# Agent attention and two expert layers: a first block of 384 tokens, another order of the first loads, and a written order from the sums to the first folded slices

## The chip, the cores and the metric

The kernel runs on one core of a Trainium2 chip. The metric is the device time of one execution in microseconds (us), the median of several runs.

## The reference, cut to what matters

```python
def attention(q, k, v, agents):                  # 12480 tokens, width 128, 49 agents, float32
    a2k = softmax(agents @ k.T / sqrt(128))      # 49 x 12480
    agent_v = a2k @ v                            # 49 x 128
    q2a = softmax(q @ agents.T / sqrt(128))      # 12480 x 49
    return q2a @ agent_v                         # 12480 x 128

x = attention(q, k, v, agents)
h = x @ w_in1                                    # 128 -> 2048
x = where(h > 0, h, exp(min(h, 0)) - 1) @ w_out1 # 2048 -> 128
h = x @ w_in2
out = (max(h, 0) + alpha * min(h, 0)) @ w_out2
```

## The kernel before, in words

The tokens are cut into 25 blocks (`BLOCKS`, L23: ten of 480, fifteen of 512). Before any block can start, the kernel must have the 49 rows of agent values. The **prologue** (L438) makes them. It reads k in ten pieces (`PIECES`, L24), computes scores per piece (S, `scores`, L471), the maximum over the first five pieces and over the last five (D and X), subtracts it and takes exp (E, `weigh`, L506), and sums the values (A, `values`, L514, the matmuls of L521). In parallel it brings in the four expert matrices in 16 slices of 512 KB (w0 to w15) and **decodes** each (`decode`, L327): the words of a slice become a high and a low float32r part by about five operations on DVE (L344 to L353), some on ACT (L340, L363, L406) and some on POOL (L373 to L409). Slices 0 to 3 are the first matrix, 4 to 7 the second; then the third and fourth matrix alternate.

After the sums A9 the two halves are put together and divided (`cs`, `avs`, `rs`, L545 to L562), turned (L564) and copied to `avn` and `avq` (L568 to L571). Then the agent values are **folded** into the first expert matrix: four slices j, each with matmuls (L578, L583), two copies by ACT to `hi` (L584, L585) and two operations on DVE (L586, L590). The result `s1`, `s1q` is the stationary side of the first layer, so that the attention's second half and the first layer are one matmul per tile of 128 hidden columns.

For each block, the **query steps** (`Q_STEPS`, L270, 17 steps) make the softmax over the agents; the last, `q_place` (L261), copies parts of it across partitions by five DMAs, on the ACT queue for block 0 and on the SP queue for all others. Then **slots** follow (`slot`, L703). One call handles two units `u` (a unit is two of a block's 16 hidden tiles, 8 units per block): the first layer `g1` (L609, L612), its activation (L619, L620, L627, L629, L636, L638), the second layer `g2` into the bank `y`, and ten units later (`L2`) the third and fourth layer, `g3` and `g4`, the latter into the bank `o`. All large products are split into three float32r matmuls (`mm3`, L431).

What sets the order: SP's queue runs in the order in which the program emits (`PINNED`). `pump` (L288) issues the loads in the order of `LOADS` (L35); it stops at the first item whose ring has no free buffer. The rings are 9 tiles for k and v and `RAW` = 6 buffers for w; a w buffer comes free with the fifth DVE operation of its decode, a k tile with its scores, a v tile with its sums. `ORDER` (L39) writes out the prologue's steps; T2 advances the decodes by two pieces (`micro`, L415), Q2 makes two query steps of block 0. For the other engines a planner, with its own model of times, orders instructions by priority, which follows the program's order but for `high_priority`: 20 for S, D, X, E and A, and `URGENT` = 400 for all from `cs` to the fourth folded slice. From slot 12 on (`AUTO`) every engine runs in program order. In the slots each of four `ask` calls (L714) advances the decodes by `MICRO` = 2 pieces. From the fold on a decode takes its PSUM scratch by `spare` (L410) from the one bank `o`, which `g4` of block 0 needs too.

Of the kernel before, what the change touches and what calls it, by code (L numbers as in the profile page):

```python
# [8 lines left out]
F32 = mybir.dt.float32  # L9
# [13 lines left out]
BLOCKS = [480] * 10 + [512] * 15  # L23
# [10 lines left out]
RAW = 6  # L34
# [4 lines left out]
    k0 q0 w0 k1 k2 w1 k3 k4 w2 k5 k6 w3 k7 k8 w4 k9 v0 w5 v1 v2 w6 v3 v4 w7 v5 v6 w8 v7 v8 w9 v9 a0 q1  # L39
# [3 lines left out]
    S0 T2 S1 Q2 T2 S2 Q2 S3 T2 Q2 S4 D0 Q2 T2 S5 X0 E0 Q2 S6 T2 E1 Q2 S7 E2 T2 S8 Q2 E3 T2 Q2 S9 D1 E4 A0 X1 A1 T2  # L43
    E5 A2 E6 T2 A3 E7 A4 E8 T2 A5 E9 T2 A6 T2 A7 T2 A8 T2 A9 Q1 T2
# [3 lines left out]
URGENT = 400  # L48
# [8 lines left out]
def agent_attention_moe_kernel(  # L57
# [378 lines left out]
    w1 = {}  # L436

    def prologue():  # L438
# [6 lines left out]
        nc.vector.tensor_scalar(out=low, in0=low, scalar1=-1.0, scalar2=None, op0=ALU.mult)  # L445
        stages = [f for k in sorted(Q_STEPS) for f in Q_STEPS[k]]
        with tc.tile_pool(name="att", bufs=1) as att:
            att2 = att
            with tc.tile_pool(name="kv", bufs=KV) as kv:
                rings["kv"] = kv  # L450
                across = bank("o", 1)
                S = att.tile([P, 10, 10, A], F32, name="S")
                pm = att.tile([P, 2, A], F32, name="pm")
                top = att.tile([P, 10, A], F32, name="top")
                mc = att.tile([A, 2], F32, name="mc")
                mb = att.tile([A, P], F32, name="mb")
                mx = {}
                for j in range(4):
                    w1[j] = att.tile([P, 4, P], F32, name=f"w1_{j}")
                pump()  # L460

                for t in range(2):
                    nc.scalar.copy(out=agd[:, t, :], in_=agp[:, :A])
                nc.scalar.copy(out=ag1[:, 0, :], in_=agp)
                nc.vector.tensor_tensor(out=ag1[:, 1, :], in0=agp, in1=ag1[:, 0, :].bitcast(F32), op=ALU.subtract)
                nc.scalar.copy(out=ag2[:, 0, :], in_=agp)
                nc.vector.memset(ag2[:, 1, :].bitcast(F32), 0.0)
                ag = agd.rearrange("p t a -> p (t a)")
                av = {}

                def scores(i):  # L471
                    _, nch, m = PIECES[i]
                    sp = hpair()
                    s4 = sp[:m, :, :10 * A].rearrange("p b (c a) -> p b c a", a=2 * A)[:, :, :, :A]
                    for c in range(nch):
                        o = sp[:m, c // 5, 2 * A * (c % 5):2 * A * (c % 5) + 2 * A]
                        nc.tensor.matmul(o, kt[i][:, c * m:(c + 1) * m], ag, start=True, stop=True)  # L477
                    del kt[i]
                    free["kv"] += 1
                    pump()  # L480
                    parts = [(slice(0, 10), s4)]
                    if nch < 10:
                        parts = [(slice(0, 5), s4[:, :1]), (slice(5, nch), s4[:, 1:, :nch - 5])]
                    for cs, part in parts:
                        def shaped(x):
                            return x[:m, cs, :].rearrange("p (b c) a -> p b c a", b=part.shape[1])
                        nc.scalar.copy(out=shaped(S[:, i]), in_=part)
                        if i % 5:
                            last = S[:, i - 1] if i % 5 == 1 else top
                            nc.vector.tensor_tensor(out=shaped(top), in0=part, in1=shaped(last), op=ALU.max)  # L490
                    if i % 5 == 4:
                        nc.vector.tensor_reduce(
                            out=pm[:, i // 5, :], in_=top.rearrange("p c a -> p a c"), axis=AX.X, op=ALU.max
                        )

                def max_down(h):
                    tp = across[:A, P * (2 + h):P * (3 + h)]
                    nc.tensor.transpose(tp, pm[:, h, :], ident)
                    nc.vector.tensor_reduce(out=mc[:, h:h + 1], in_=tp, axis=AX.X, op=ALU.max)
                    nc.vector.tensor_copy(out=mb, in_=mc[:, h:h + 1].to_broadcast([A, P]))  # L500

                def max_across(h):
                    mx[h] = across[:, P * h:P * h + A]
                    nc.tensor.matmul(mx[h], mb, ident[:A, :A], start=True, stop=True)

                def weigh(i):  # L506
                    _, nch, m = PIECES[i]
                    nc.vector.tensor_tensor(
                        out=S[:m, i, :nch, :], in0=S[:m, i, :nch, :],
                        in1=mx[i // 5][:m, :].unsqueeze(1).to_broadcast([m, nch, A]), op=ALU.subtract,  # L510
                    )
                    nc.scalar.activation(out=S[:m, i, :nch, :], in_=S[:m, i, :nch, :], func=AF.Exp, scale=SCALE)

                def values(i):  # L514
                    _, nch, m = PIECES[i]
                    h, first, last = i // 5, i % 5 == 0, i % 5 == 4
                    if i == 0:
                        y = bank("y", 1)
                        av.update({n: y[:, 256 * n:256 * n + P + 1] for n in range(2)})
                    for c in range(nch):  # L520
                        nc.tensor.matmul(  # L521
                            av[h][:A, 0:P + 1], S[:m, i, c, :], vt[i][:m, c, :],
                            start=(first and c == 0), stop=(last and c == nch - 1),
                        )
                    del vt[i]
                    free["kv"] += 1
                    pump()

                def query(n):
                    for _ in range(n):  # L530
                        stages.pop(0)(0)

                does = {"S": scores, "D": max_down, "X": max_across, "E": weigh, "A": values, "Q": query, "T": micro}
                for x in ORDER.split():
                    if x[0] in "SDXEA":
                        with tc.high_priority(offset=PRIORITY):
                            does[x[0]](int(x[1:]))
                    else:
                        does[x[0]](int(x[1:]))
                assert not stages and all(i in done for i in range(4)), (stages, done, started)  # L540

                urgent = tc.high_priority(offset=URGENT)
                urgent.__enter__()

                cs = att.tile([A, 4], F32, name="cs")  # L545
                nc.vector.tensor_tensor(out=cs[:, 2:3], in0=mc[:, 0:1], in1=mc[:, 1:2], op=ALU.max)
                nc.vector.tensor_scalar(out=cs[:, 0:2], in0=mc, scalar1=cs[:, 2:3], scalar2=None, op0=ALU.subtract)
                nc.scalar.activation(out=cs[:, 0:2], in_=cs[:, 0:2], func=AF.Exp, scale=SCALE)
                avs = att.tile([A, 2, P + 1], F32, name="avs")
                nc.vector.tensor_scalar(  # L550
                    out=avs[:, 0, :], in0=av[0][:A, 0:P + 1], scalar1=cs[:, 0:1], scalar2=None, op0=ALU.mult
                )
                nc.vector.scalar_tensor_tensor(
                    out=avs[:, 1, :], in0=av[1][:A, 0:P + 1], scalar=cs[:, 1:2], in1=avs[:, 0, :],
                    op0=ALU.mult, op1=ALU.add,
                )
                rs = att.tile([A, 1], F32, name="rs")
                nc.vector.tensor_scalar(out=rs, in0=avs[:, 1, P:P + 1], scalar1=1e-9, scalar2=None, op0=ALU.add)
                nc.vector.reciprocal(out=rs, in_=rs)
                nc.vector.tensor_scalar(  # L560
# [13 lines left out]
            for j in range(4):  # L574
# [7 lines left out]
                for g in range(4):  # L582
                    nc.tensor.matmul(hq[32 * g:32 * g + 32, :], avq[:, g, :], w1[j][:, g, :], start=True, stop=True)  # L583
# [201 lines left out]
```

## Time and profile before

| | us |
|---|---|
| median of 3 runs | 1138.63 (1138.54 to 1139.36) |
| the profiled execution, whole time | 1139.54 |
| its span, first to last instruction | 1137.6 |
| PE busy in the span | 1087.1 (96%) |
| DVE busy | 863.8 (76%) |
| ACT busy | 804.1 (71%) |
| POOL busy | 612.3 (54%) |

PE is TensorE, DVE VectorE, ACT ScalarE, POOL GpSimd, SP SyncE; an engine's name with a q is its queue issuing DMAs. A busy time is a share of the whole span, so it hides that the first 160 us look quite unlike the rest. The matmuls' ends are modelled, so a busy PE is not always one at its peak.

### The profile page before, as it was taken

The numbers are of one execution on the slowest core, as the hardware profiler recorded it, in microseconds if no ns is written. First come the engines' busy times: TensorE is split into PE (matmuls) and PEld (weight loads), VectorE is DVE, ScalarE is ACT, GpSimd is POOL, SyncE is SP. The second block draws the span as 40 slices with busy tenths as digits, with TensorE's granted clock in tenths as the row PEclk, the third lists the DMA queues.
The fourth block names the chain that finished last, engine by engine and source line by source line (L and its number), as shares of the span: only waits on it lengthen the run. The fifth ranks groups of instructions, "written<-read, shape, count | busy, mean of one in ns | idle before, by whom it ended". The sixth has DMA issues, their size and how long they took to land.

```text
span 1137.6 us, 13427 instructions
## 1 busy us (share of the span) xinstructions
PE 1087.1 (96%) x5012; PEld 854.6 (75%) x5012; DVE 863.8 (76%) x995; ACT 804.1 (71%) x921; POOL 612.3 (54%) x340
## 2 busy tenths in 40 slices
PE   7677769999999999999999999999999999999998
PEld 7664558888888888877777777777777777777776
DVE  5679947878787878788787887878878778778653
ACT  3347637777877777777777777777777777877753
POOL 2326635655565556565555655665556555565440
PEclk9879679999999999999999999999999999999999
DMA  9940000000000000000000000000000000000000
GB/s 352 295 136 1 18 0 27 18 27 9 19 26 19 18 19 28 18 19 19 28 10 19 28 10 28 19 19 19 19 27 12 19 29 10 19 19 17 12 1 18
DMA packets 28978, 41.33 MB, mean 36 GB/s; under 512 B 3329, under 2 KB 19669, under 8 KB 28915
## 3 DMA queue, kind: packets, MB, share of 16 engines
q1 hardware_dynamic: 28719, 40.24, 11.5%
q8 instruction: 39, 0.64, 0.2%
q10 hardware_dynamic: 196, 0.25, 0.1%
q14 instruction: 24, 0.20, 0.1%
HBM read 27.60 MB, written 6.39 MB: 30 GB/s over the span
## 4 chain that ended last, share of the span: by engine, by line
PE 91%; DVE 4%; DMA 2%; ACT 2%; POOL 1%; issue 1%; SPq 0%; DVEq 0%; ACTq 0%; POOLq 0%
PE o L432 10%; PE o L434 9%; PE o L433 9%; PE h L433 8%; PE h L434 8%; PE h L432 8%; PE y L433 8%; PE y L432 8%; PE y L434 8%; PE h L609 8%; PE h L612 4%; PE y L521 2%; PE h L477 1%; DMA vt<-in_vm_dram 1%; DMA kt<-in_kT_dram 1%
## 5 line engine op out<-in xcount | busy, mean ns | idle before, releaser
L638 POOL TENSOR_TENSOR gl<-g,gh 128x1024 fp32r<-128x1024 f32 (+1 forms) x200 | 468.0, 2345 | 279.1 <-DVE gh L629 176.4
L669 DVE SCALAR_TENSOR_TENSOR xl<-h,xh 128x1024 fp32r<-128x1024 f32 (+1 forms) x200 | 239.6, 1198 | 144.8 <-ACT xh L668 143.4
L668 ACT ACTIVATE xh<-h 128x1024 fp32r<-128x1024 f32 (+1 forms) x200 | 201.2, 1006 | 193.1 <-PE h L434 192.6
L627 DVE SCALAR_TENSOR_TENSOR g<-e,h 128x1024 f32<-128x1024 f32 (+1 forms) x200 | 236.4, 1182 | 75.6 <-ACT e L620 54.9
L619 ACT ACTIVATE e<-h 128x1024 f32<-128x1024 f32 (+1 forms) x200 | 199.4, 997 | 36.5 <-PE h L612 33.3
L620 ACT ACTIVATE e<-e 128x1024 f32<-128x1024 f32 (+1 forms) x200 | 207.7, 1039 | 6.2
L432 PE MATMUL o<-xh,wo2h 128*128 128x512 f32 (+1 forms) x400 | 166.0, 415 | 0.4 <-DVE lin L394 0.4
L433 PE MATMUL y<-gl,wo1h 128*128 128x512 f32 (+1 forms) x400 | 157.5, 394 | 4.0 <-POOL gl L638 4.0
L432 PE MATMUL h<-yh,wi2h 128*128 128x512 f32 (+1 forms) x400 | 156.0, 390 | 2.7 <-ACT yh L656 2.7
L432 PE MATMUL y<-gh,wo1h 128*128 128x512 f32 (+1 forms) x400 | 157.4, 394 | 0.0
L433 PE MATMUL o<-xl,wo2h 128*128 128x512 f32 (+1 forms) x400 | 156.3, 391 | 0.7 <-DVE xl L669 0.7
L434 PE MATMUL y<-gh,wo1l 128*128 128x512 f32 (+1 forms) x400 | 156.8, 392 | 0.0
L434 PE MATMUL o<-xh,wo2l 128*128 128x512 f32 (+1 forms) x400 | 156.7, 392 | 0.0
L433 PE MATMUL h<-yl,wi2h 128*128 128x512 f32 (+1 forms) x400 | 156.3, 391 | 0.0
L434 PE MATMUL h<-yh,wi2l 128*128 128x512 f32 (+1 forms) x400 | 155.8, 389 | 0.0
L629 DVE SCALAR_TENSOR_TENSOR gh<-e,h 128x1024 fp32r<-128x1024 f32 (+1 forms) x100 | 118.8, 1188 | 0.0
L609 PE MATMUL h<-pst,s 128*128 128x512 f32 (+1 forms) x400 | 110.7, 396 | 5.6 <-DVE g L627 2.3
L636 ACT CAST gh<-g 128x1024 fp32r<-128x1024 f32 (+1 forms) x100 | 102.0, 1020 | 5.5 <-DVE g L627 5.5
L432 PEld LDWEIGHTS o<-xh,wo2h 128*128 128x128 f32 x400 | 75.7, 189 | 35.0 <-ACT xh L668 16.9
L609 PEld LDWEIGHTS h<-pst,s 128*128 128x128 f32 x400 | 75.2, 190 | 23.9 <-issue 2.6
L433 PEld LDWEIGHTS y<-gl,wo1h 128*128 128x128 f32 x400 | 76.1, 190 | 21.8 <-POOL gl L638 5.6
L432 PEld LDWEIGHTS h<-yh,wi2h 128*128 128x128 f32 x400 | 75.2, 188 | 18.9 <-ACT yh L656 2.9
(144 smaller groups left out, 1315.0 us busy)
## 6 DMA issues: line engine op xcount, KB each, us to landing
vt<-in_vm_dram SPq DMA_DIRECT2D x9, 640.0 KB
kt<-in_kT_dram SPq DMA_DIRECT2D x8, 640.0 KB
wi<-in_w_in_dram SPq DMA_DIRECT2D x8, 512.0 KB
wo<-in_w_out_dram SPq DMA_DIRECT2D x8, 512.0 KB
q<-in_qT_dram SPq DMA_DIRECT2D x15, 256.0 KB
psq<-pst SPq DMA_DIRECT2D x60, 64.0 KB
out_dram<-o SPq DMA_DIRECT2D x15, 256.0 KB
q<-in_qT_dram SPq DMA_DIRECT2D x10, 240.0 KB
```

What stands on the lines that cost most here:

```text
L432: nc.tensor.matmul(out, w_hi, x_hi, start=start, stop=False)
L433: nc.tensor.matmul(out, w_hi, x_lo, start=False, stop=False)
L434: nc.tensor.matmul(out, w_lo, x_hi, start=False, stop=stop)
L609: nc.tensor.matmul(h_t[u + v][:, c, :], s1[:, i + 2 * v + c, :], pst[b][:, :n], start=True, stop=False)
L619: nc.scalar.activation(out=e, in_=h_t[u], func=AF.Relu, scale=-1.0)
L620: nc.scalar.activation(out=e, in_=e, func=AF.Exp, scale=-1.0)
L627: nc.vector.scalar_tensor_tensor(out=g, in0=e, scalar=-1.0, in1=h, op0=ALU.add, op1=ALU.max)
L629: nc.vector.scalar_tensor_tensor(out=gh, in0=e, scalar=-1.0, in1=h, op0=ALU.add, op1=ALU.max)
L636: nc.scalar.copy(out=gh, in_=g)
L638: nc.gpsimd.tensor_tensor(out=gl, in0=g, in1=gh.bitcast(F32), op=ALU.subtract)
L668: nc.scalar.activation(out=xh, in_=h, func=AF.Relu)
L669: nc.vector.scalar_tensor_tensor(out=xl, in0=h, scalar=0.0, in1=xh.bitcast(F32), op0=ALU.max, op1=ALU.subtract)
```

## The change

The first block has 384 tokens, followed by six of 480 and eighteen of 512: 25 blocks as before. `LOADS` asks for w0 ahead of k0, and for w1 to w5 earlier among the k; `RAW` falls to 4. `ORDER` begins with one T2 and has one less at the end, and the last query step of block 0 (Q1) moves from the end to behind E6. `q_place` issues on SP for block 0 too. The tiles `w1`, `avn` and `avq` move to the permanent pool, `avq` keeps one copy instead of four, `hi` has one buffer, the output tile `o` one instead of two. What followed the sums becomes `normalize` and `fold(j)`; `normalize`, `fold(0)` and `fold(1)` stand in a region in which every engine keeps program order, without `URGENT`; `fold(2)` and `fold(3)` come behind slot 0, and slot 0 advances no decode. The bodies of the prologue's steps only lose indentation.

```diff
-BLOCKS = [480] * 10 + [512] * 15
+BLOCKS = [384] + [480] * 6 + [512] * 18
...
-RAW = 6
+RAW = 4
...
 LOADS = """
-    k0 q0 w0 k1 k2 w1 k3 k4 w2 k5 k6 w3 k7 k8 w4 k9 v0 w5 v1 v2 w6 v3 v4 w7 v5 v6 w8 v7 v8 w9 v9 a0 q1
+    w0 k0 w1 k1 q0 w2 k2 w3 k3 w4 k4 k5 w5 k6 k7 w6 k8 k9 v0 v1 w7 v2 v3 v4 w8 v5 v6 w9 v7 v8 v9 a0 q1
     w10 w11 w12 w13 w14 w15
 """
 ORDER = """
-    S0 T2 S1 Q2 T2 S2 Q2 S3 T2 Q2 S4 D0 Q2 T2 S5 X0 E0 Q2 S6 T2 E1 Q2 S7 E2 T2 S8 Q2 E3 T2 Q2 S9 D1 E4 A0 X1 A1 T2
-    E5 A2 E6 T2 A3 E7 A4 E8 T2 A5 E9 T2 A6 T2 A7 T2 A8 T2 A9 Q1 T2
+    T2 S0 T2 S1 Q2 T2 S2 Q2 S3 T2 Q2 S4 D0 Q2 T2 S5 X0 E0 Q2 S6 T2 E1 Q2 S7 E2 T2 S8 Q2 E3 T2 Q2 S9 D1 E4 A0 X1 A1 T2
+    E5 A2 E6 T2 Q1 A3 E7 A4 E8 T2 A5 E9 T2 A6 T2 A7 T2 A8 T2 A9
 """
...
-        eng = nc.sync if b else nc.scalar
         for g in range(4):
-            eng.dma_start(out=psq[b][32 * g:32 * g + 32, :n].bitcast(F32), in_=pst[b][Q0:A, :n].bitcast(F32))
-        eng.dma_start(out=pst[b][P - 15:P - 30 + Q0, :n].bitcast(F32), in_=pst[b][15:Q0, :n].bitcast(F32))
+            nc.sync.dma_start(out=psq[b][32 * g:32 * g + 32, :n].bitcast(F32), in_=pst[b][Q0:A, :n].bitcast(F32))
+        nc.sync.dma_start(out=pst[b][P - 15:P - 30 + Q0, :n].bitcast(F32), in_=pst[b][15:Q0, :n].bitcast(F32))
...
+    w1 = [const.tile([P, 4, P], F32, name=f"w1_{j}") for j in range(4)]
+    avn = const.tile([P, 2, AP], F32, name="avn")
+    avq = const.tile([P, 32], F32, name="avq")
...
-                urgent = tc.high_priority(offset=URGENT)
-                urgent.__enter__()
...
-                nc.vector.tensor_copy(out=avn[:, :, :A], in_=at[:, 0:A].unsqueeze(1).to_broadcast([P, 2, A]))
-                nc.scalar.copy(out=avq, in_=at[:, Q0:A].unsqueeze(1).to_broadcast([P, 4, 32]))
-                nc.vector.tensor_copy(out=avn[:, 0, A:], in_=at[:, 0:15])
-                nc.scalar.copy(out=avn[:, 1, A:A + Q0 - 15], in_=at[:, 15:Q0])
+        nc.vector.tensor_copy(out=avn[:, :, :A], in_=at[:, 0:A].unsqueeze(1).to_broadcast([P, 2, A]))
+        nc.vector.tensor_copy(out=avn[:, 0, A:], in_=at[:, 0:15])
+        nc.vector.tensor_copy(out=avn[:, 1, A:A + Q0 - 15], in_=at[:, 15:Q0])
+        nc.scalar.copy(out=avq, in_=at[:, Q0:A])
...
-            hi = [att2.tile([P, 5, P], F32R, name=f"hi{j}") for j in range(2)]
-            for j in range(4):
...
+    def fold(j):
...
+        hi = dec.tile([P, 5, P], F32R, tag="hi", bufs=1, name="hi")
...
-            ot = work.tile([P, BLK], F32, tag="o", bufs=2, name="o")
+            ot = work.tile([P, BLK], F32, tag="o", bufs=1, name="o")
...
-    with tc.manual_schedule(engines=PINNED):
-        prologue()
+    with tc.tile_pool(name="att", bufs=1) as att:
+        with tc.tile_pool(name="kv", bufs=KV) as kv:
+            rings["kv"] = kv
+            with tc.manual_schedule(engines=PINNED):
+                sums = prologue(att)
+        with tc.manual_schedule():
+            normalize(att, *sums)
+            for j in range(2):
+                fold(j)
...
         def ask(k):
-            micro(MICRO)
+            if s:
+                micro(MICRO)
...
     with tc.manual_schedule(engines=PINNED):
         for s in range(0, AUTO, 2):
             slot(s)
+            if s == 0:
+                fold(2)
+                fold(3)
```

## Rows read from the trace of the kernel before

**Rows 1.** The page, busy tenths of PE in 40 slices of 28.4 us.

```profile
PE   7677769999999999999999999999999999999998
```

**Rows 2.** Busy time by stretch of the first 160 us: stretch, length, each engine, granted clock, DMA share, GB/s.

```profile
0.00:9.80 9.80, 4.56 (x20) 4.34 (x20) 0.72 (x6) 3.33 (x9) 1.90 (x7) 1.00 0.77 253
9.80:40.90 31.10, 29.04 (x208) 27.48 (x209) 26.77 (x50) 11.04 (x20) 9.04 (x17) 1.00 1.08 368
40.90:49.30 8.40, 6.07 (x55) 5.82 (x53) 0.01 (x1) 0.91 (x3) 0.00 (x0) 1.00 1.11 294
49.30:59.30 10.00, 1.01 (x3) 0.66 (x3) 9.88 (x20) 4.00 (x8) 5.09 (x4) 0.59 1.03 252
59.30:72.00 12.70, 12.70 (x92) 12.45 (x92) 12.40 (x22) 7.01 (x13) 6.26 (x5) 0.79 0.61 211
72.00:75.00 3.00, 3.00 (x28) 2.81 (x27) 0.00 (x1) 0.00 (x0) 0.00 (x0) 1.00 0.11 46
75.00:90.50 15.50, 9.89 (x55) 3.97 (x56) 11.24 (x26) 5.90 (x14) 2.38 (x3) 0.78 0.11 34
90.50:131.00 40.50, 29.82 (x106) 19.09 (x106) 38.13 (x57) 29.03 (x38) 30.36 (x19) 0.83 0.05 13
131.00:151.00 20.00, 14.58 (x54) 9.95 (x54) 18.08 (x23) 14.79 (x19) 12.00 (x7) 0.81 0.00 1
151.00:160.00 9.00, 3.26 (x13) 2.56 (x13) 5.27 (x9) 0.09 (x1) 4.04 (x4) 0.50 0.00 0
```

**Rows 3.** The chain that ended last, from 38 us: start, length, what.

```profile
38.08 9.23 DMA vt<-in_vm_dram
47.38 1.23 DMA pst<-pst
...
59.40 15.57 PE y L521 x116
```

**Rows 4.** Timeline of ACT and its queue, 41 to 50 us: start, length, instruction.

```profile
41.96 3.22 ACTq L266 DMA_DIRECT2D psq<-pst  x2
47.38 1.12 ACTq L267 DMA_DIRECT2D pst<-pst  x1
48.60 0.66 ACT L340 ACTIVATE da<-wo 128x512 f32<-128x512 f32 x1 [7.49 <-DMA pst<-pst]
...
49.67 0.36 ACT L487 COPY S<-h 120x245 f32<-120x245 f32 x1
```

**Rows 5.** Timeline of the first 10 us: who first uses k0, q0 and w0.

```profile
4.07 4.56 PE L477 MATMUL h<-agd,kt 128*128 128x98 f32 x20 [4.07 <-DMA kt<-in_kT_dram]
...
6.49 0.59 ACT L148 CAST qh<-q 128x480 fp32r<-128x480 f32 x1 [3.12 <-DMA q<-in_qT_dram]
...
9.10 0.66 ACT L340 ACTIVATE da<-wi 128x512 f32<-128x512 f32 x1 [2.02 <-DMA wi<-in_w_in_dram]
...
9.79 0.69 DVE L344 TENSOR_SCALAR h<-da 128x512 f32<-128x512 f32 x1 [6.31 <-ACT da L340]
```

**Rows 6.** Waits of SP's queue for a decode: total us, times, longest.

```profile
SPq L308 <- DVE da L353: 18.1, 3, 7.8
```

**Rows 7.** Timeline of PE from the second folded slice to the first slot.

```profile
85.58 0.43 PE L583 MATMUL h<-w,avq 128*32 128x128 f32 x8
...
90.52 0.68 PE L609 MATMUL h<-pst,s 128*128 128x480 f32 x2 [0.16 <-PE h L157]
```

**Rows 8.** DVE groups by form, 90.5 to 160 us: the first layer's activation.

```profile
L627 DVE SCALAR_TENSOR_TENSOR g<-e,h 128x960 f32<-128x960 f32 x14 | 16.0, 1140 | 0.1
L629 DVE SCALAR_TENSOR_TENSOR gh<-e,h 128x960 fp32r<-128x960 f32 x7 | 8.0, 1143 | 0.0
```

**Rows 9.** Busy time by stretch in the blocks of 480 and of 512.

```profile
300.00:400.00 100.00, 100.00 (x470) 81.08 (x469) 79.03 (x89) 76.84 (x89) 57.52 (x32) 1.00 0.06 18
900.00:1000.00 100.00, 100.00 (x443) 77.45 (x442) 78.28 (x87) 77.14 (x85) 57.95 (x30) 1.00 0.06 19
```

**Rows 10.** Timeline: the decodes' products in the bank `o`, first and last, and the fourth layer.

```profile
85.94 0.94 PE L390 MATMUL o<-dg,da 128*128 128x128 f32 x6
...
159.59 0.29 DVE L394 TENSOR_TENSOR lin<-lin,o 128x128 f32<-128x128 f32 x1 [2.17 <-PE o L390]
...
159.93 0.77 PE L432 MATMUL o<-xh,wo2h 128*128 128x480 f32 x1 [0.38 <-DVE lin L394]
```

More of the change, by code (lines that the diff above doesn't have):

```diff
@@ L434, in mm3, with prologue @@
         nc.tensor.matmul(out, w_lo, x_hi, start=False, stop=stop)
-    w1 = {}
-    def prologue():
+    w1 = [const.tile([P, 4, P], F32, name=f"w1_{j}") for j in range(4)]
+    avn = const.tile([P, 2, AP], F32, name="avn")
+    avq = const.tile([P, 32], F32, name="avq")
+    def prologue(att):
         nc.sync.dma_start(out=agp, in_=agT)
@@ L445, in prologue @@
         nc.vector.tensor_scalar(out=low, in0=low, scalar1=-1.0, scalar2=None, op0=ALU.mult)
+        nc.vector.memset(avn[:, 1, A:], 0.0)
         stages = [f for k in sorted(Q_STEPS) for f in Q_STEPS[k]]
[L447 to L457, printed above, removed]
[L458 to L593 removed]
@@ new lines, in prologue @@
+        across = bank("o", 1)
+        S = att.tile([P, 10, 10, A], F32, name="S")
+        pm = att.tile([P, 2, A], F32, name="pm")
+        top = att.tile([P, 10, A], F32, name="top")
+        mc = att.tile([A, 2], F32, name="mc")
+        mb = att.tile([A, P], F32, name="mb")
+        mx = {}
+        pump()
+        for t in range(2):
+            nc.scalar.copy(out=agd[:, t, :], in_=agp[:, :A])
+        nc.scalar.copy(out=ag1[:, 0, :], in_=agp)
+        nc.vector.tensor_tensor(out=ag1[:, 1, :], in0=agp, in1=ag1[:, 0, :].bitcast(F32), op=ALU.subtract)
@@ new lines, in prologue, with scores, shaped @@
+        nc.scalar.copy(out=ag2[:, 0, :], in_=agp)
+        nc.vector.memset(ag2[:, 1, :].bitcast(F32), 0.0)
+        ag = agd.rearrange("p t a -> p (t a)")
+        av = {}
+        def scores(i):
+            _, nch, m = PIECES[i]
+            sp = hpair()
+            s4 = sp[:m, :, :10 * A].rearrange("p b (c a) -> p b c a", a=2 * A)[:, :, :, :A]
+            for c in range(nch):
+                o = sp[:m, c // 5, 2 * A * (c % 5):2 * A * (c % 5) + 2 * A]
+                nc.tensor.matmul(o, kt[i][:, c * m:(c + 1) * m], ag, start=True, stop=True)
+            del kt[i]
+            free["kv"] += 1
+            pump()
+            parts = [(slice(0, 10), s4)]
+            if nch < 10:
+                parts = [(slice(0, 5), s4[:, :1]), (slice(5, nch), s4[:, 1:, :nch - 5])]
+            for cs, part in parts:
+                def shaped(x):
+                    return x[:m, cs, :].rearrange("p (b c) a -> p b c a", b=part.shape[1])
+                nc.scalar.copy(out=shaped(S[:, i]), in_=part)
+                if i % 5:
+                    last = S[:, i - 1] if i % 5 == 1 else top
+                    nc.vector.tensor_tensor(out=shaped(top), in0=part, in1=shaped(last), op=ALU.max)
+            if i % 5 == 4:
+                nc.vector.tensor_reduce(
+                    out=pm[:, i // 5, :], in_=top.rearrange("p c a -> p a c"), axis=AX.X, op=ALU.max
+                )
@@ new lines, in values @@
+        def values(i):
+            _, nch, m = PIECES[i]
+            h, first, last = i // 5, i % 5 == 0, i % 5 == 4
+            if i == 0:
+                y = bank("y", 1)
+                av.update({n: y[:, 256 * n:256 * n + P + 1] for n in range(2)})
+            for c in range(nch):
+                nc.tensor.matmul(
+                    av[h][:A, 0:P + 1], S[:m, i, c, :], vt[i][:m, c, :],
+                    start=(first and c == 0), stop=(last and c == nch - 1),
+                )
+            del vt[i]
+            free["kv"] += 1
+            pump()
@@ new lines, in query @@
+        def query(n):
+            for _ in range(n):
+                stages.pop(0)(0)
+        does = {"S": scores, "D": max_down, "X": max_across, "E": weigh, "A": values, "Q": query, "T": micro}
+        for x in ORDER.split():
+            if x[0] in "SDXEA":
+                with tc.high_priority(offset=PRIORITY):
+                    does[x[0]](int(x[1:]))
+            else:
+                does[x[0]](int(x[1:]))
+        assert not stages and all(i in done for i in range(4)), (stages, done, started)
@@ new lines, in fold @@
+    def fold(j):
+        hp = hpair()
+        w4 = hp[:, 0, :].rearrange("p (f c) -> p f c", c=P)
+        hq = hp[:, 1, :P]
+        nc.tensor.matmul(
+            hp[:, 0, :], avn.rearrange("p j a -> p (j a)"), w1[j].rearrange("p f c -> p (f c)"), start=True, stop=True
+        )
+        for g in range(4):
+            nc.tensor.matmul(hq[32 * g:32 * g + 32, :], avq, w1[j][:, g, :], start=True, stop=True)
+        hi = dec.tile([P, 5, P], F32R, tag="hi", bufs=1, name="hi")
+        nc.scalar.copy(out=hi[:, :4, :], in_=w4)
+        nc.scalar.copy(out=hi[:, 4, :], in_=hq)
+        nc.vector.scalar_tensor_tensor(
+            out=s1[:, 4 * j:4 * j + 4, :], in0=hi[:, :4, :].bitcast(F32), scalar=low, in1=w4, op0=ALU.mult, op1=ALU.add
+        )
+        nc.vector.tensor_tensor(out=s1q[:, j, :], in0=hq, in1=hi[:, 4, :].bitcast(F32), op=ALU.subtract)
```

59 lines of the change are left out of this document (33 added, 26 removed).

## The prediction

> **What bounds the kernel now.** I read the busy tenths first: PE is full from the seventh slice to the end and at six or seven tenths before it [rows 1]. The number of blocks, of matmuls per block and of columns stays the same under the change, so the full part keeps its length but for small terms, and the question is when it begins. The table by stretch answers that [rows 2]. From 9.8 to 151 us DVE is the engine that is nearly always busy: 116.5 us of the 141.2 (the eight rows from 9.80:40.90 to 131.00:151.00 added). What it does there (decode 16 slices, prepare scores, activate the first units) must be done before PE can run full. Its idle time is 24.7 us: 4.3 up to 40.9, 8.4 at 40.9 to 49.3, 0.4 up to 72, 3.0 at 72 to 75, 4.3 at 75 to 90.5, 4.3 up to 151. So I treat the start as a DVE account: first operation, work, idle time.
>
> The chain of waits names the largest hole. It runs through a transfer of v, then the last placing transfer of block 0, and then 15.57 us of sums [rows 3]. ACT's timeline shows why: ACT issues the placing transfers itself, stands in those issues from 41 us on, does no work for 7.49 us, and the last pieces' scores are copied only at 49.67 [rows 4]. DVE waits for ACT, the second maximum comes late, and the sums that need it run as one lump to 75.
>
> **The change, part by part.**
>
> *Placing transfers on SP.* ACT no longer stands, so the 8.4 us of DVE idle go. On SP the five issues stand behind w10, which is behind v9, so no k or v is behind them; w11 to w15 are, and those are wanted only after the fold. psq is wanted by the first slot, some 10 us later than the sums' end. I count 0 on SP; if w11 came so late that its decode waited, it would cost at most the 8.4 again, since nothing longer was seen. What the Trainium skill, "DMA: Bandwidth & Descriptors", section "Issuing engines are not separate DMA queues", says speaks against the full gain: transfers of all issuers share the same engines, and another issuer saves only the issue time. By that I would credit the two issues drawn in those rows, 3.22 + 1.12 = 4.3 us, and arrive 4.1 us later than with 8.4. I take 8.4, because the row shows ACT empty for the whole stretch and its next instruction released by the transfer.
>
> *w0 first.* k0's first part (with the agents 288 KB) was used at 4.07, q0 (912 KB in order) at 6.49, w0 (1424 KB) at 9.10, DVE started at 9.79 [rows 5]. Now w0 ends at 544 KB. Between the first two points that is 4.07 + 256/258 = 5.1; with ACT's 0.66 before it and the rest of a hand-over DVE starts at 5.9, 3.9 earlier. Not before 4.8 (if w0 lands with 4.07), not after 9.8.
>
> *RAW of 4, and the order of k and w.* From w4 on SP waits until the decode four slices back frees a buffer, and k4, k5 and all that follow are queued behind that wait. What must land before the last sum is unchanged: k and v 6.39 MB each, w0 to w9 5.24, q0, agents and placing 0.5, together 18.55 MB; by 59.3 us 18.9 had moved (253, 368, 294 and 252 GB/s over their stretches [rows 2]), so v9 landed near 58, an estimate. DVE has work until about 65 before it needs the sums, since decodes 8 to 10 are now all placed ahead of them (10 operations of about 0.7 beyond the 49 us that it had done by 75). So DVE covers the transfers, and a wait of SP costs nothing while it is shorter than some 5 us. SP did wait for decodes before, three times, 7.8 us at most [rows 6]: that is the other end. I take 0.
>
> *T2 in front, one less behind; Q1 earlier.* The number of decode steps is the same. 0.
>
> *Sums to folded slices.* Before, all four slices stood ahead of the first slot on PE: it could have begun at 86.0, behind the second slice, and began at 90.52 [rows 7]. So up to 4.5 us of latency go. The copy that moves from ACT to DVE adds 0.2 us of DVE work; `hi` with one buffer makes the second slice's ACT copies wait for the first's DVE operations, about 1 us that slot 0's matmuls cover. The work of slices 2 and 3 is only moved. In the account I shorten the 4.3 idle of this stretch to 2.5, and the 3.0 spent waiting for the last sum to 1.5 (its other ends are 0 and 4.3, 0 and 3.0, as the transfers come).
>
> *No decode step in slot 0.* Moves work later, changes no sum; where it hurts is a rival below.
>
> *384 tokens.* The activation takes 24.0 us for 14 units [rows 8], 1.71 per unit; on 8 units a fifth less is 2.7 us off DVE's account. The 96 tokens come back in later blocks. PE's pitch is 100/470 = 213 ns at 480 columns and 100/443 = 226 at 512 [rows 9], 0.40 ns per column, so 96 columns are 39 ns. Layers 1 and 2 of a block have 80 matmuls (32 and 48), and what is moved of them from a stretch bound by DVE to one bound by PE costs 80 x 39 ns = 3.1 us. Layers 3 and 4 run in the full part either way: 0, unless the weight loads do not fit under 384 columns (pitch then not below 213: 100 x 39 ns = 3.9 us more, the upper bound).
>
> *Output tile with one buffer.* A block lasts some 41 us (181 matmuls at 226 ns), so the tile is long sent when it is wanted again: 0.
>
> **Sum.** Start 5.9, work 116.5 - 2.7 + 0.2 = 114.0, idle 2.5 + 1.5 + the 9.0 in small gaps = 13.0: DVE's stage ends at 132.9 instead of 151, 18.1 earlier. Less 3.1 of moved PE work: 15.0. The profiled execution took 1139.54, so 1124.5; the median stands 0.9 below it: **1123.5**. With the bounds of the idle terms and of the start it is 1119 to 1128. A measurement of this kernel can tell about 0.2% (2.3 us) from no change.
>
> **Rivals.**
>
> *Only the issue time is saved* (the rule above): what held ACT is in part something else that stays. 1123.5 + 4.1 = 1127.6. Against it: ACT's next instruction is released by that transfer. Chance 0.08.
>
> *SP waits for decodes.* RAW of 4 puts k and v behind decodes; one wait of 7.8 that lands on v9 delays the sums by as much, and DVE covers little of it if its decodes are what is late: about 1131. For it: SP did wait so. Against: DVE starts earlier and w0 to w3 need no wait. Two such waits give 1138.6. Chance 0.14, of which 0.04 for no change.
>
> *The written order keeps nothing out.* It fixes only the order among its own instructions; decode operations may still stand between them, as they may without it. Then the 1.8 us that I took off that stretch stay: 1125.3. Chance 0.07.
>
> *The chain through the bank `o` decides, and it is slower.* The decodes after the fold share one bank, from 85.94 to 159.59, and the fourth layer of block 0 waits for its end [rows 10]; it took 73.7 us. Now it starts only with slot 2. If slot 0 and the folds behind it take the 12.5 us that the first two units' work took before, starting at 72 and a little more for two folds, the chain starts near 86 and, as long as before, ends near 160; with the 3.1 us moved the time is 1142. It decides once the last product comes after 156.5. Against: each decode in it needs only some 6 us, the rest is waiting for a DVE busy with other work, and that work shrinks. Chance 0.09.
>
> *The end of the stage closes too.* From 151 to 160 DVE is busy 5.3 of 9.0 us and PE 3.3, on the last decode alone. Were that decode done among other work, 8 us more go: 1115.5. Nothing in the change orders it so. Chance 0.12.
>
> **Numbers.** My forecast has 0.50, as 1119 to 1128. Faster: 0.50 + 0.08 + 0.10 + 0.07 + 0.12 = 0.87; same 0.04; slower 0.09. The range goes from 1112 (the last rival with a start at 4.8 and the shorter idle terms) to 1133 (SP's wait with 2 us more); it leaves out the slower case, two SP waits, and the thin ends of the others.
>
> **What would show it.** Right: no placing transfer on ACT's queue and no gap in ACT or DVE at 41 to 49; DVE's first decode operation near 6; the sums ending by about 62 and the first L609 near 72; the fourth layer starting near 142; the rest of the span as long as before plus 3. Wrong: long SP waits for L353 before v9; the fourth layer still starting near 160 behind L394; a pitch in block 0 that does not fall with its columns.

## The result, and the profile after

The changed kernel took 1114.26 us (median of 4, 1111.96 to 1114.83) against 1138.99 (1138.54 to 1139.97) for the kernel before in the same comparison: ratio 0.9778, interval 0.9761 to 0.9795. The span fell from 1137.6 to 1112.5 us, by 25.1.

The tenths look almost as before [rows 1]; of the first seven slices two are two tenths fuller and one is a tenth emptier. What the page can't show is where the 25.1 went:

```profile
PE   7877689999999999999999999999999999999998
```

The start of the fourth layer of block 0 cuts the span in two. It is the same instruction in every kernel here, with 4385 matmuls from it to the end. These rows are of the timeline of PE, after: the sums, the turning of the agent values, the first slot, the fourth layer.

```profile
50.38 14.70 PE L516 MATMUL y<-vt,S 128*49 128x129 f32 x116
...
69.88 0.31 PE L555 MATMUL o<-ident,avs 49*128 49x49 f32 x1 [4.22 <-DVE avs L553]
...
76.61 0.60 PE L594 MATMUL h<-pst,s 128*128 128x384 f32 x2
...
147.38 0.69 PE L430 MATMUL o<-xh,wo2h 128*128 128x384 f32 x1 [0.38 <-DVE lin L392]
```

Before, the fourth layer started at 159.93 [rows 10]: the **start** became 12.55 us shorter. The **rest**, from there to the end, went from 977.65 to 965.13, another 12.5. Busy time by stretch for the rest alone, before:

```profile
159.90:1138.00 978.10, 973.28 (x4385) 765.50 (x4385) 741.34 (x787) 728.13 (x802) 541.29 (x277) 1.00 0.06 19
```

and after, with the stretch of 900 to 1000 below it:

```profile
147.30:1113.00 965.70, 960.60 (x4385) 763.15 (x4385) 748.36 (x788) 732.42 (x802) 545.81 (x277) 1.00 0.07 19
...
900.00:1000.00 100.00, 100.00 (x452) 78.22 (x451) 80.72 (x86) 77.77 (x85) 58.48 (x29) 1.00 0.07 19
```

The number of matmuls is the same, PE is full and its granted clock is 1.00 in both, yet PE is busy 12.7 us less. In the same 100 us of blocks of 512 it now issues 452 matmuls instead of 443 [rows 9]. The timeline shows the **pitch** directly, the time from the start of one matmul to the start of the next. Three products of the third layer in a row, twice, before:

```profile
701.23 0.39 PE L432 MATMUL h<-yh,wi2h 128*128 128x512 f32 x1
...
702.39 0.39 PE L434 MATMUL h<-yh,wi2l 128*128 128x512 f32 x1
```

and after:

```profile
701.34 0.39 PE L430 MATMUL h<-yh,wi2h 128*128 128x512 f32 x1
...
702.47 0.39 PE L432 MATMUL h<-yh,wi2l 128*128 128x512 f32 x1
```

Five pitches take 1.16 us before and 1.13 after. The median distance of two starts in layers 2 to 4, from 700 to 900 us, is 232 ns before and 227 after. A row's duration (0.39) is longer than the pitch, because matmuls overlap, and to two decimals it is the same in both.

The start by stretch, after (compare [rows 2]; the columns are the same):

```profile
6.30:40.00 33.70, 31.36 (x215) 30.67 (x216) 29.96 (x56) 12.91 (x24) 10.03 (x18) 0.95 1.05 366
40.00:50.00 10.00, 7.98 (x69) 7.32 (x67) 9.18 (x19) 4.48 (x9) 7.02 (x7) 1.00 1.13 317
50.00:58.40 8.40, 8.37 (x60) 8.18 (x61) 8.32 (x16) 4.15 (x9) 2.55 (x2) 0.80 1.17 251
58.40:63.50 5.10, 5.10 (x49) 5.10 (x47) 2.56 (x5) 1.23 (x3) 2.44 (x2) 1.00 0.73 216
63.50:70.50 7.00, 2.48 (x20) 1.92 (x17) 6.32 (x16) 2.31 (x5) 0.00 (x0) 0.79 0.68 225
70.50:77.80 7.30, 7.11 (x36) 3.41 (x36) 2.66 (x8) 3.28 (x8) 1.04 (x1) 0.73 0.09 35
77.80:139.20 61.40, 42.82 (x176) 30.25 (x175) 56.81 (x83) 40.30 (x57) 38.68 (x26) 0.81 0.07 18
139.20:147.30 8.10, 3.19 (x12) 2.50 (x12) 4.41 (x7) 0.62 (x1) 4.22 (x5) 0.50 0.00 0
```

The hole of 40.9 to 49.3, in which DVE did 0.01 us of work, is gone: ACT works 4.48 us and DVE 9.18 in 40 to 50. DVE is now idle elsewhere. From its timeline, after, the operations that ended its idle times:

```profile
6.35 0.69 DVE L342 TENSOR_SCALAR h<-da 128x512 f32<-128x512 f32 x1 [2.87 <-ACT da L338]
...
59.92 0.17 DVE L315 TENSOR_SCALAR oma<-al 128x16 f32<-128x16 f32 x1 [1.60 <-DMA al<-in_alpha_dram]
...
63.57 0.69 DVE L342 TENSOR_SCALAR h<-da 128x512 f32<-128x512 f32 x1 [1.10 <-ACT da L338]
...
74.21 0.75 DVE L575 SCALAR_TENSOR_TENSOR s<-hi,low,h 128x512 fp32r<-128x512 f32 x1 [3.57 <-ACT hi L574]
```

It starts 3.4 us earlier, as was to come from w0. It then waits for the alpha transfer (1.60) and for w10 (1.10) between 58.3 and 63.6, and for the fold between 70.5 and 77.8. The longest piece of the chain of waits in the start, after, is w10's transfer; start, length, what:

```profile
54.93 7.85 DMA wi<-in_w_in_dram
```

### The profile page after: what moved, and what is told of

The parts are those of the page before. It is cut to its first block, busy times and chain, and to the rows that moved or that the text cites. A ratio compares the mean times of both kernels' runs of the same rounds, so it can differ in the third digit from the quotient of the medians.

```text
span 1112.5 us, 13438 instructions
## 1 busy us (share of the span) xinstructions
PE 1069.0 (96%) x5012; PEld 852.5 (77%) x5012; DVE 869.3 (78%) x996; ACT 804.4 (72%) x920; POOL 612.5 (55%) x340
## 4 chain that ended last, share of the span: by engine, by line
PE 87%; DVE 5%; ACT 2%; issue 1%; DMA 1%; POOL 1%; DVEq 0%; POOLq 0%; ACTq 0%
PE o L430 10%; PE o L432 8%; PE o L431 8%; PE h L594 8%; PE h L432 8%; PE h L431 8%; PE h L430 8%; PE y L430 8%; PE y L431 8%; PE y L432 7%; PE h L597 4%; DVE g L612 1%; DVE gh L614 1%; DMA wi<-in_w_in_dram 1%; PE h L155 0%
## 5 line engine op out<-in xcount | busy, mean ns | idle before, releaser
L623 POOL TENSOR_TENSOR gl<-g,gh 128x1024 fp32r<-128x1024 f32 (+2 forms) x200 | 468.4, 2347 | 270.5 <-DVE gh L614 176.6
L654 DVE SCALAR_TENSOR_TENSOR xl<-h,xh 128x1024 fp32r<-128x1024 f32 (+2 forms) x200 | 239.6, 1198 | 129.9 <-ACT xh L653 128.4
L653 ACT ACTIVATE xh<-h 128x1024 fp32r<-128x1024 f32 (+2 forms) x200 | 201.3, 1006 | 177.7 <-PE h L432 176.9
L612 DVE SCALAR_TENSOR_TENSOR g<-e,h 128x1024 f32<-128x1024 f32 (+2 forms) x200 | 236.4, 1182 | 71.8 <-ACT e L605 56.1
L604 ACT ACTIVATE e<-h 128x1024 f32<-128x1024 f32 (+2 forms) x200 | 199.2, 997 | 34.0 <-PE h L597 32.4
L605 ACT ACTIVATE e<-e 128x1024 f32<-128x1024 f32 (+2 forms) x200 | 208.0, 1040 | 6.0
L430 PE MATMUL o<-xh,wo2h 128*128 128x512 f32 (+2 forms) x400 | 164.7, 412 | 0.4 <-DVE lin L392 0.4
L431 PE MATMUL y<-gl,wo1h 128*128 128x512 f32 (+2 forms) x400 | 155.3, 388 | 1.4 <-POOL gl L623 1.4
L430 PE MATMUL y<-gh,wo1h 128*128 128x512 f32 (+2 forms) x400 | 155.2, 388 | 0.0
L431 PE MATMUL h<-yl,wi2h 128*128 128x512 f32 (+2 forms) x400 | 154.9, 387 | 0.1
```

The source lines that it names most:

```text
L430: nc.tensor.matmul(out, w_hi, x_hi, start=start, stop=False)
L431: nc.tensor.matmul(out, w_hi, x_lo, start=False, stop=False)
L604: nc.scalar.activation(out=e, in_=h_t[u], func=AF.Relu, scale=-1.0)
L605: nc.scalar.activation(out=e, in_=e, func=AF.Exp, scale=-1.0)
L612: nc.vector.scalar_tensor_tensor(out=g, in0=e, scalar=-1.0, in1=h, op0=ALU.add, op1=ALU.max)
L623: nc.gpsimd.tensor_tensor(out=gl, in0=g, in1=gh.bitcast(F32), op=ALU.subtract)
```

## The experiments

Ratios are against the kernel before, timed again beside each set of runs (its medians were 1138.99 to 1140.88); they compare better across sets than the times. From a trace of each, the start of the fourth layer ("start") and the time from there to the end ("rest") are read. Five traces of kernels whose instructions stand in the very same order (after, e2, e8, e9, e11) have starts of 147.38, 146.55, 144.51, 146.25 and 144.88. So a difference in start of under some 3 us between two single traces says nothing.

**Where the tiles lie.** The addresses at which the compiled programs place their tiles give a first theory for the rest. In before, the weights of layers 2 to 4 begin at 192 modulo 256 bytes of a partition, and the moving tiles of the slots (e, g, gh, gl, yh, yl, xh, xl) at 64. After, both begin at 192: `w1`, `avn` and `avq` in the permanent pool add 8832 bytes below the slots' tiles, two raw buffers fewer take 8192 away, and `hi` adds 2560, in all 3200 = 12 x 256 + 128. The change made two things equal that were 128 apart, and nobody asked for it. The rival: the smaller first block, or the timing of the slots, made the pitch. To test it, one small tile that nobody fills to its end grows by 128 bytes, in before (e1) and in after (e2):

```diff
-        return sm.tile([AP, BLK // 32], F32, tag=tag, name=tag)
+        return sm.tile([AP, BLK // 32 + (32 if tag == "r" else 0)], F32, tag=tag, name=tag)
```

> The kernel before, with one small tile of the query steps made 128 bytes longer, so that the tiles behind it (pst, psq and all of the slots' tiles: e, g, gh, gl, yh, yl, xh, xl, o) begin 128 bytes further in SBUF. Order and work are the same. Layout theory: the changed kernel's full part is faster because its moved tiles begin 192 bytes past a multiple of 256, as the weight tiles do, and no longer 64. Then the pitch of matmuls of 512 columns falls from 232 to about 227 ns here too, the fourth layer still starts near 160, and the time falls by 13 to 18 us to 1121 to 1126. Rival, order theory: the pitch comes from the changed order or from the single output buffer; then this stays at 1138 to 1140 with 232 ns.

> The changed kernel with the same 128 bytes more, so that the slots' tiles begin 64 bytes past a multiple of 256. Layout theory: the pitch at 512 columns rises from 227 to about 232 ns, the fourth layer still starts near 147, and the time rises by 13 to 18 us to 1127 to 1132. Order theory: 1113 to 1115 and 227 ns. If only the distance modulo 512 counts, it is something between the two.

Measured: e1 took 1125.05 us (1124.49 to 1126.8), ratio 0.9867 (0.9851 to 0.9884); e2 1129.27 (1128.8 to 1130.31), ratio 0.9907 (0.9892 to 0.9922). The rest of e1, busy time by stretch:

```profile
160.80:1123.30 962.50, 958.46 (x4385) 763.65 (x4385) 743.25 (x787) 727.89 (x802) 541.46 (x277) 1.00 0.07 19
```

and of e2:

```profile
146.50:1128.00 981.50, 976.32 (x4385) 764.88 (x4385) 746.30 (x787) 731.71 (x802) 545.82 (x277) 1.00 0.06 19
```

The pitch is 227 ns in e1 and 232 in e2. The same 128 bytes take 14.7 us off the rest of before (977.65 to 962.96) and add 16.7 to the rest of after (965.13 to 981.83). No instruction, no order and no transfer differs. The rest's gain is the layout's. And e2 is the change with the layout of before: in it the edits themselves are worth 0.9%, 10.7 us (1139.95 less 1129.27).

Is it the slots' address alone, or the two against each other? e8 moves the weights and the slots' tiles by 128 bytes, so that both are at 64; e11 moves the weights by 128 and the slots' tiles by 512, so that they are at 64 and 192.

```diff
-    low = const.tile([P, 1], F32, name="low")
+    low = const.tile([P, 40], F32, name="low")[:, :1]
```

e11 has this line too, and 96 elements in place of e2's 32.

> The changed kernel with 128 bytes more in a small tile ahead of the weights, so that the weights of layers 2 to 4 and all tiles behind them, the slots' too, begin 128 bytes further: both 64 past a multiple of 256. If it counts that the two operands of a matmul begin alike modulo 256, the pitch at 512 columns stays at 227 ns (1113 to 1116). If the place of the moving tiles alone counts, it is 232 ns (1128 to 1131), as with only those shifted.

> The changed kernel with the weights of layers 2 to 4 128 bytes further (64 past a multiple of 256) and the slots' tiles where they were modulo 512 (192 past 256). If like places count, the pitch at 512 columns is 232 ns and the time 1128 to 1131. If the place of the moving tiles alone counted, 227 ns and 1112 to 1115.

Measured in one run each: e8 1112.68 us, pitch 227 ns; e11 1126.82, pitch 232. The rest of e8:

```profile
144.50:1109.70 965.20, 961.09 (x4385) 763.72 (x4385) 748.12 (x787) 731.94 (x802) 545.53 (x277) 1.00 0.07 19
```

and of e11:

```profile
144.80:1124.50 979.70, 975.51 (x4385) 763.93 (x4385) 746.52 (x788) 732.21 (x802) 545.94 (x277) 1.00 0.07 19
```

So 192 beside 192 and 64 beside 64 are quick, 192 beside 64 is slow whichever of the two is where: it is the place of the one operand against the other. The granted clock is 1.00 in all of these rows.

The first layer still runs at 233 ns after: its weights `s1` lie at 160, its moving tile `pst` at 192. e9 moves `s1` by 32 bytes and the rest by 256, so that all lie at 192:

```diff
-    oma = const.tile([P, NF], F32, name="oma")
+    oma = const.tile([P, NF + 8], F32, name="oma")[:, :NF]
...
-    low = const.tile([P, 1], F32, name="low")
+    low = const.tile([P, 64], F32, name="low")[:, :1]
```

> The changed kernel with 32 bytes more ahead of s1 and s1q (192 past a multiple of 256 instead of 160, as pst is) and 224 more behind them, so that weights and slots' tiles stay alike modulo 256. If like places of the two operands modulo 256 count down to 32 bytes, the first layer's pitch falls from 233 to 227 ns at 512 columns and, with 16 such matmuls in each of 25 blocks, the rest behind the fourth layer's start gets some 2 us shorter: 1111.5 to 1113. Rival: it counts in steps of 64 or 128 bytes and the first layer's pitch has another cause: 233 ns, 1113 to 1115.

Measured: 1115.11 us (1114.32 to 1115.74), ratio 0.9787 (0.9764 to 0.9809), no gain over after. The first layer's pairs do go from 233 to 227 ns, but the rest stays:

```profile
146.20:1112.00 965.80, 960.85 (x4385) 764.02 (x4385) 747.46 (x787) 731.97 (x802) 545.10 (x277) 1.00 0.07 19
```

By groups, from 700 to 900 us, the mean distance to the next start rose elsewhere (first products of the fourth layer 255.2 to 257.0 ns, second ones 226.6 to 229.4). Why is open: a quicker first layer may only arrive earlier at a wait.

**The placing transfers.** In e7 the kernel before gets this part of the change alone; e3 is after with it undone.

```diff
-        eng = nc.sync if b else nc.scalar
+        eng = nc.sync
```

> The kernel before with the placing transfers of block 0 on SP, nothing else. There the step stands last on SP, behind w15, so psq comes late. Theory: ACT's stand at 41 to 49 us is worth most of the 9.7 us by which the sums and the first slot were earlier; the sums end 5 to 8 us earlier, and the time falls by 4 to 9 us, to 1130 to 1135, if psq then does not hold the first slot. Rival: the gap is taken by other waits (the transfers of v) and only 1 to 2 us go, as putting them back cost 1.4: 1137 to 1139. Second rival: psq behind the late loads holds the first slot: 1139 or more.

> The changed kernel with the placing transfers of block 0 back on ACT's queue. Theory: ACT stands in the issues for 5 us or more while v is loaded, DVE loses about as much, and the fourth layer starts 4 to 8 us later: 1118 to 1122. Rival: in the new order the issues fall where ACT has nothing urgent, below 1 us: 1114 to 1115. The pitch stays at 227 ns.

Measured: e7 1131.29 us (1129.2 to 1133.26), ratio 0.992 (0.9902 to 0.9938); e3 1115.64 (1114.77 to 1116.55), ratio 0.9786 (0.9772 to 0.9801). In e7's busy time by stretch the hole is filled (DVE 8.28 where it had 0.01), and the fourth layer starts at 149.58:

```profile
40.90:49.30 8.40, 5.97 (x53) 5.59 (x51) 8.28 (x16) 3.12 (x7) 5.10 (x4) 1.00 1.11 316
```

```profile
149.58 0.77 PE L432 MATMUL o<-xh,wo2h 128*128 128x480 f32 x1 [0.38 <-DVE lin L394]
```

That is 10.35 us earlier than before, with a rest of 977.53, as before. So alone it is worth most of the start's 12.55. In e3 its absence costs only 0.8 at the fourth layer (148.15), within the spread. ACT's timeline of e3 shows why:

```profile
30.09 1.24 ACTq L265 DMA_DIRECT2D psq<-pst  x2
...
32.91 0.51 ACTq L265 DMA_DIRECT2D psq<-pst  x1
...
35.23 0.51 ACTq L265 DMA_DIRECT2D psq<-pst  x1
...
37.12 1.12 ACTq L266 DMA_DIRECT2D pst<-pst  x1
...
41.95 0.36 ACT L483 COPY S<-h 120x245 f32<-120x245 f32 x1
```

With the other parts of the change in place the issues fall from 30 to 38 us, ahead of the last scores' copies, and no issue holds ACT for 3.22 us as in [rows 4]; DVE is busy 9.84 us of 40 to 50. So one and the same hole goes by the move to SP alone (e7) and by the other parts without it (e3). Which of the other parts moved the issues was not tried by itself.

**Layout and placing together, on the kernel before** (e12, the edits of e7 and e1):

> The kernel before with two edits alone: the placing transfers of block 0 on SP, and the slots' tiles 128 bytes further. If these two make up the whole gain, the fourth layer starts near 149.6, the rest lasts 963 us, and the time is 1113 to 1117, level with the changed kernel. If the other parts of the change (loads, written order, first block) carry some of it, it stays above by that: 1118 or more.

Measured: 1115.74 us (1114.39 to 1116.62), ratio 0.979 (0.9769 to 0.981); start 149.74, rest 964.16. Its fourth layer and its rest:

```profile
149.74 0.77 PE L432 MATMUL o<-xh,wo2h 128*128 128x480 f32 x1 [0.38 <-DVE lin L394]
```

```profile
149.70:1113.50 963.80, 959.66 (x4385) 764.52 (x4385) 743.38 (x787) 728.20 (x802) 541.62 (x277) 1.00 0.07 19
```

Two edited lines give 2.1% where the whole change gives 2.2%, and the intervals overlap. It is the same in the slow layout, where e7 (0.992) stands beside e2 (0.9907) with intervals that overlap. So next to these two, the loads, `RAW`, the written order and the first block add nothing that stands clear of the noise.

**The first block** (e4, after with the blocks of before):

```diff
-BLOCKS = [384] + [480] * 6 + [512] * 18
+BLOCKS = [480] * 10 + [512] * 15
```

> The changed kernel with the blocks of before (ten of 480, fifteen of 512). Theory of the prediction: the start, bound by DVE, gets 2.7 us longer and the rest 3.1 us shorter, together 0: 1113 to 1116, the fourth layer starting near 150. Rival: the first block's size is what shortened the start, and the time rises by 4 us or more, to above 1118.

Measured: 1114.74 us (1114.39 to 1115.28), ratio 0.9779 (0.9764 to 0.9793): the same as after. The smaller first block starts the fourth layer 2.5 us earlier (149.90 to 147.38) and pays 2.75 in the rest (962.38 to 965.13). The rests of like kernels differ by less than that (965.13, 965.65 and 966.14 in after, e8 and e9; 980.01 and 981.83 in e11 and e2), so the second is seen, though not to a fraction of a microsecond; the first lies within the spread of single traces.

**The written order** (e5, after with the fold as before: all four slices ahead of slot 0, by priority, and decode steps in slot 0):

```diff
-        with tc.manual_schedule():
+        with tc.manual_schedule(engines=PINNED), tc.high_priority(offset=400):
             normalize(att, *sums)
-            for j in range(2):
+            for j in range(4):
...
-            if s:
-                micro(MICRO)
+            micro(MICRO)
...
-            if s == 0:
-                fold(2)
-                fold(3)
```

> The changed kernel with the step from the sums to the folds as before: no written order but on SP, priority 400, all four folded slices ahead of the first slot, and decodes in slot 0. Theory: the first slot's matmuls then wait for all four slices and begin 3 to 5 us later behind the last sum, and the fourth layer 2 to 5 us later than 147: 1116 to 1119. Rival: what is bound is DVE's account, to which the order of the folds adds nothing; then the fourth layer starts within 1 us of 147: 1113 to 1115.5. The pitch stays at 227 ns.

Measured: 1116.09 us (1114.48 to 1117.34), ratio 0.9791 (0.9775 to 0.9807). PE's timeline:

```profile
82.14 0.98 PE L594 MATMUL h<-pst,s 128*128 128x384 f32 x2 [1.46 <-issue]
...
146.78 0.69 PE L430 MATMUL o<-xh,wo2h 128*128 128x384 f32 x1 [0.38 <-DVE lin L392]
```

and its busy time by stretch over the fold:

```profile
70.50:82.10 11.60, 8.70 (x50) 3.91 (x50) 5.59 (x12) 4.37 (x10) 3.14 (x3) 0.79 0.02 7
```

Without the written order the first slot starts 5.5 us later. DVE is idle for 6.0 us around the fold (11.60 - 5.59) where it is idle for 4.6 in after (70.5 to 77.8). That is a gain of 1.4 in the account. At the fourth layer it isn't seen (146.78 against 147.38, within the spread), and the ratios' intervals overlap. So an earlier first slot is worth little by itself. The likely reason, not tested alone, is that DVE has the same work left up to the fourth layer.

**The list of loads.** e6 is after with the list and the place of the T2 step of before; e13 takes back the list alone and leaves T2 at the head. The diff shows the heads of the two lines; e13 has the first pair only.

```diff
-    w0 k0 w1 k1 q0 w2 k2 w3 k3 w4 k4 k5 w5 k6 k7 w6 k8 k9 v0 v1 w7 v2 v3 v4 w8 v5 v6 w9 v7 v8 v9 a0 q1
+    k0 q0 w0 k1 k2 w1 k3 k4 w2 k5 k6 w3 k7 k8 w4 k9 v0 w5 v1 v2 w6 v3 v4 w7 v5 v6 w8 v7 v8 w9 v9 a0 q1
...
-    T2 S0 T2 S1 Q2
+    S0 T2 S1 Q2
...
-    A5 E9 T2 A6 T2 A7 T2 A8 T2 A9
+    A5 E9 T2 A6 T2 A7 T2 A8 T2 A9 T2
```

> The changed kernel with the load list of before (k0 and q0 ahead of w0) and the T2 at the end of the step list instead of at its head; RAW stays 4. Theory: DVE starts its first decode 3.5 us later, near 9.8, and the fourth layer starts 3 to 6 us later: 1117 to 1121. Rival: DVE has slack later in the prologue that takes it up, below 1 us: 1114 to 1115.5.

> The changed kernel with the load list of before alone; the T2 stays at the head of the steps. Five traces of programs with the changed kernel's order of instructions had the fourth layer start between 144.5 and 147.4, so the 144.75 without list and T2 may be the list's cost or the spread. If the list costs some 2 us: fourth layer 143 to 145, ratio to the kernel before below 0.9765. If the list is worth what the prediction gave it (DVE starting 3.5 us earlier): 149 to 151 and a ratio near 0.981. If neither, 144 to 148 and 0.976 to 0.980.

Measured: e6 1112.89 us (1109.75 to 1114.09), ratio 0.9755 (0.9737 to 0.9773); e13 1117.22 (1115.97 to 1124.39, 5 runs), ratio 0.9827 (0.9799 to 0.9854). The fourth layer, e6:

```profile
144.75 0.69 PE L430 MATMUL o<-xh,wo2h 128*128 128x384 f32 x1 [0.38 <-DVE lin L392]
```

and e13, with the last turning of a maximum ahead of the sums:

```profile
56.65 0.66 PE L499 MATMUL o<-ident,mb 49*128 49x49 f32 x2
...
148.22 0.69 PE L430 MATMUL o<-xh,wo2h 128*128 128x384 f32 x1 [0.38 <-DVE lin L392]
```

In e6 DVE's first decode starts at 9.34, 3 us later than after, and the sums end at 62.97, 2.1 earlier. From its first decode to the fourth layer DVE is idle for 16.4 us in e6 and for 20.8 in after, and that makes up for the later start. So the early w0 gains nothing here. List and step belong together, since e13, with T2 at the head and w0 late, has its maximum 6.6 us later than after (56.65 against 50.03). Its sums end 5.7 us later (70.79 against 65.08), yet its fourth layer only 0.8: the end of the sums does not set the fourth layer one for one. e6 has the lowest time of all, but its interval overlaps that of after: a version that beats the change beyond doubt was not found.

## Why the prediction was right, and where its steps were not

The time and the sign came out inside the range, 9 us below the point. Two errors of opposite sign stand behind that: the fourth layer came 5.5 us later than forecast (147.4 against "near 142"; the sums ended at 65.1 against "about 62", the first slot began at 76.6 against "near 72"), and the rest was 12.5 us shorter instead of 3.1 longer. That the time fell between 1112 and 1119 is luck: the range reached there for a rival that did not come. What the forecast summed up, the edits without a new layout, is e2: 10.7 us saved instead of 15, with 1129.27 at the upper edge of the 1119 to 1128 that had the chance of 0.50.

- **"The full part keeps its length but for small terms": failed.** It was argued from equal numbers of blocks, matmuls and columns. That leaves the pitch, which I took as a function of the columns alone. (Its 213 and 226 ns were means over all matmuls, those of L612 included, which start in groups with a median of 3.5 ns from one to the next; from start to start the layers' pitch before was 220 and 232.) At equal counts e1 and e2 move the rest by 15 to 17 us with 128 bytes. The rows at hand gave no price for it: before showed one layout only. What could have been seen ahead is that the change moves tiles between pools and changes a ring, hence every address above them.
- **The small term itself held**, within the spread of the rests: blocks +3.1 forecast, +2.75 in e4, and +4.2 between the slow layouts (977.65 to 981.83).
- **Placing on SP: right.** 8.4 forecast, 10.35 at the fourth layer, and 9.6 us between the medians of e7 and of before beside it (1131.29 against 1140.88). The Trainium skill, "DMA: Bandwidth & Descriptors", section "Issuing engines are not separate DMA queues", says that issuing from several engines saves only the sequencer's time for the issue; the prediction's estimate by it was 4.3. e7 speaks against reading that as an upper bound on what a compute engine gets back: in the hole ACT stood, and DVE with it (0.01 of 8.4 us busy before, 8.28 in e7). The rival of that rule fell in e7. The price of the placing could not have been read from the finished change, where e3 shows only 0.8 at the fourth layer.
- **The DVE account: right in kind, 6.3 us short.** Forecast: start 5.9, work 114.0, idle 13.0, end of the stage 132.9; it came at 139.2, and the stretch behind it was 0.8 shorter than before, which leaves the 5.5 above. By the rows of after, from 6.3 to 139.2: start 6.35, work 115.8 (the seven rows' DVE added), idle 17.1. Of the excess of 4.1 in idle, the fold's share did not fall from 4.3 to 2.5 but came to 4.6 (7.30 - 2.66), and 2.5 are new at 58.4 to 63.5: some 1.5 for alpha, whose operation stands in DVE's order ahead of further decode work, and 1.0 for w10, when DVE had run out of decodes. The prediction had named such a wait for w11 only, and counted 0; alpha it did not name.
- **The start of DVE: size right (6.35 against 5.9), worth wrong.** DVE's earlier first operation was counted 1:1 in its account. e6 starts 3 us later and its fourth layer comes no later, because DVE is idle for less behind it.
- **SP waiting for decodes: it came, ahead of v9, and cost nothing that the runs show.** Waits of SP's queue up to 70 us, after:

```profile
SPq L306 <- DVE da L351: 33.3, 6, 17.7
```

  The 7.8 of [rows 6], which the prediction took as the price of one wait, held no k or v: all three waits before lie behind the last v (asked for at 51.93). After, the longest, 17.7, begins at 68.5, behind the sums. The other five, 15.6 us together, lie ahead of v9, which the prediction had called a sign of being wrong. The longest of these lies between the first two of these rows of SP's timeline:

```profile
13.89 0.91 SPq L296 DMA_DIRECT2D kt<-in_kT_dram  x2
23.37 0.33 SPq L306 DMA_DIRECT2D wo<-in_w_out_dram  x1
...
48.76 3.14 SPq L302 DMA_DIRECT2D vt<-in_vl_dram  x1
...
54.93 0.36 SPq L306 DMA_DIRECT2D wi<-in_w_in_dram  x1
```

  and before, for the last v and w10:

```profile
51.93 1.10 SPq L304 DMA_DIRECT2D vt<-in_vl_dram  x1
...
55.06 0.35 SPq L308 DMA_DIRECT2D wi<-in_w_in_dram  x1
```

  From 14.8 to 23.3 the DMA engines moved 414 GB/s of what had been asked for until then, against 419 in the same stretch of the kernel before. The last v was asked for 3.2 us earlier than before, and the sums ended 9.9 us earlier (65.08 against 74.96). w10 was asked for at 54.93, as before (55.06), and no decode held that request; it landed at 62.8, and DVE, further ahead than before, stood for it.
- **The written order, 1.8 in the account: not settled.** Against its absence (e5) it saves 1.4 us of DVE's idle time, near the 1.8, and moves the first slot by 5.5 us (the forecast had up to 4.5 of latency); at the fourth layer nothing is seen of it. The rival "keeps nothing out" differs by too little for single traces to decide.
- **384 tokens, 0: right** (1114.74 in e4 against 1114.26; -2.5 at the fourth layer and +2.75 behind it).
- **The slower case** (the chain through the bank `o`) did not come: it would have ended near 160. **The end of the stage** did not close either: from 139.2 to 147.3 DVE is busy 4.41 of 8.1 us, as open as before. That its time, 1115.5, lies near the result is chance.

## What to carry to other kernels

When a profile shows one engine full, compare its pitch per instruction (starts in the timeline, matmuls per 100 us), not its busy share: here the share was 96% before and after, and 12.5 us lay in the pitch. When a change moves or resizes tiles, list the addresses before and after, and test the shift alone by padding one small tile; otherwise its gain or loss is credited to the edits. And undo a part both from the old and from the new kernel: a part worth 10 us alone was worth about 1, no more than the noise, where the other parts had removed the same hole.

## What the runs showed of the hardware that I had not expected

The pitch of float32r matmuls of 512 columns with 128 x 128 weights depends on where weights and moving tile begin relative to each other modulo 256 bytes: 227 ns at equal places (192/192 in after, e1 and e12, 64/64 in e8), 232 at 128 apart (192/64 in before, e2 and e7, 64/192 in e11). For 480 columns it is 217 (after and e1, 300 to 400 us) and 220 (before and e2). The first layer at 512 columns, 32 or 96 bytes apart, took 232 to 234, and 227 when both lay at 192 (e9). At 227 ns for 512 columns and about 176 for the 384 of the first block, 0.40 ns per column between these two stays right, as the prediction had it. What in the chip makes the difference, and which distances count, was not settled: only equal places, 32, 96 and 128 apart were run, and 256 was not told apart from a larger modulus (equal places here are equal modulo 512 too).
